# Turning a unit's row maxima on VectorE in 32x32 blocks instead of on TensorE, in a gated attention and MLP kernel

## The chip, the cores and the metric

The kernel runs on one core of a Trainium2 chip. The metric is the device time of one launch in microseconds (us). Before the change it is 2267.89 us, the median of three runs (2267.58 to 2268.26).

## What is computed

The input is 2048 tokens of width 576. A multi-head softmax attention (32 heads of width 18) and an MLP with a LayerNorm ahead of it are computed from the same `x`, and a sigmoid gate mixes them:

```python
x = A_x
g = _sigmoid((x * gate_w).sum(-1, keepdims=True))
# a: softmax attention
q, k, v = ...                       # x @ wqkv, H = 32 heads, Dh = 18
scores = jnp.einsum("bhqd,bhkd->bhqk", q, k) * Dh ** -0.5
p = _softmax(scores, axis=-1)
a = jnp.einsum("bhqk,bhkd->bhqd", p, v) ... @ wo
# b: MLP
y = _layernorm(x, axis=-1)
h = _gelu(jnp.einsum("bsd,df->bsf", y, w1) + b1)
b = jnp.einsum("bsf,fd->bsd", h, w2) + b2
return g * a + (1 - g) * b
```

The change concerns only the softmax: the maximum of each row of `scores`, which is taken off before the exponential.

## The kernel before

**Two passes over the scores.** The kernel works through 32 units. A unit is a pair of heads and one half of the queries: 2 heads, 1024 queries in 8 tiles of 128, and all 2048 keys. The scores of a unit are computed twice. The first pass (`s1_round`, the matmul of line 204) puts 128 queries on the partitions and 512 keys along the row, and VectorE reduces each result to one maximum per query (line 206). A round `(u, r)` is one such tile for both heads; a unit has 32 rounds. The second pass (`s2`, the matmul of line 284) puts 128 keys on the partitions and 512 queries along the row, ScalarE takes the exponential straight from PSUM (line 286), and `pv` multiplies the result with the values (line 313).

**How the maximum gets into the second pass.** The second pass has queries along the row, where a value per query can't be a bias. So it contracts over 56 rows and not 54: the tile `qa` has two more rows per head, 54 and 55 (and 118 and 119 for the second head, which lies from partition 64), that hold minus the maximum, as a rounded part and its remainder, and `ka` has ones there. `s1_finish` makes these values on VectorE (lines 215 to 218) as a tile `nm2` of 128 queries by 32 columns; the columns are head (2), part (2) and query tile (8). They lie down the partitions, and `qa` wants them along a row. The inner function `rows` does that: TensorE turns the 128x32 tile to 32x128 in a PSUM bank (line 222), ScalarE copies it to the SBUF tile `mr` (line 224), and four DMAs, one for each head and part, each move 8 rows of 512 bytes into one row of `qa` (lines 228 to 237, by way of the helper at line 114).

**PSUM.** The bank for the turned tile comes from the pool `ps_s1`, three banks which are otherwise those of the first pass. A matmul of the first pass therefore needs a bank that VectorE has reduced, or, after a turn, that ScalarE has copied. The second pass has two banks of its own (`ps_s2`), the MLP two (`ps_w`), the output of `pv` one.

**The order of the work** is written out by hand. All engines run the instructions in the order in which the program emits them. The main loop goes over 512 steps (unit and key tile `kc`). A step has two halves; each half emits one round of the first pass between the two heads of the second, then a part of the MLP (`fill`: matmuls of lines 553 and 685), and every second step a `pv`. The first pass runs ahead by some steps: the last round of a unit is emitted about four steps ahead of the first `s2` that needs its maxima. The function `run_due` counts slots; `defer(n, fn)` runs `fn` when n more slots have gone by, and most halves and MLP pieces are a slot each. `s1_finish` runs one slot after a unit's last round. In the loop, `rows` is then put in the list `ROWS`, which is emptied right after the next `pv` (lines 1350 to 1352); for the first unit, whose maxima are made ahead of the loop, `rows` is deferred by 8 slots.

**DMA queues.** Nearly all DMAs are issued from SyncE's queue (SP), in program order: a DMA that waits holds back those behind it. While the loads of the next block of normalized input (`load_y`, tile `big`) stand in that queue, which is so for two of the units, the flag `aside` sends the stores of `rows` to ScalarE's queue instead, spread over slots with `defer`.

The names in the rows below: `nm` is `nm2`, `m` the maxima of a unit, `ps` any PSUM bank, `p` and `ring` the buffers of exponentials, `w` the weights' two parts, `x` a raw or accumulated tile, `z` and `zz` the MLP's activations.

Of the kernel before, what the change touches and what calls it, by code (L numbers as in the profile page):

```python
# [9 lines left out]
F32 = mybir.dt.float32  # L10
F32R = mybir.dt.float32r
AF = mybir.ActivationFunctionType
# [5 lines left out]
P = 128  # L18
# [41 lines left out]
def gated_mix_kernel(ctx: ExitStack, tc: tile.TileContext, x, wqkv, wo, w1, b1, w2, b2, gate_w, out):  # L60
    nc = tc.nc
# [18 lines left out]
    ident = const.tile([P, P], F32, name="ident")  # L80
# [12 lines left out]
    asm = ctx.enter_context(tc.tile_pool(name="asm", bufs=2))  # L93
    ps_s1 = ctx.enter_context(tc.tile_pool(name="ps_s1", bufs=NS1, space=PSUM))
# [5 lines left out]
    def psum(pool):  # L100
        return pool.tile([P, TB], F32, name="ps")
# [10 lines left out]
    def dma_r(queue, dst, src):  # L112

        queue.dma_start(dst.bitcast(F32), src)
# [5 lines left out]
    def defer(n, fn):  # L120
        later.append((slot[0] + n, fn))
# [11 lines left out]
    aside = [-1]  # L133

    def run_due(ns=SLOT):

        slot[0] += 1
        now[0] += ns
        if chain and chain[0][0]():
            chain.pop(0)[1]()  # L140
        due = [f for t, f in timed if t <= now[0]]
        timed[:] = [(t, f) for t, f in timed if t > now[0]]
        for f in due:
            f()
        due = [f for s, f in later if s <= slot[0]]
        later[:] = [(s, f) for s, f in later if s > slot[0]]
        for f in due:
            f()
        k = 0
        while k < len(bg):  # L150
            if pool_end[0] - now[0] < bg[k][2] and slot[0] >= bg[k][0]():
                bg.pop(k)[1]()
                k = 0
            else:
                k += 1
# [15 lines left out]
    def load_q(u):  # L171
        pair, half = unit(u)
        qa = QA[u % 3]
        for h in range(2):
            d0 = (2 * pair + h) * DH
            for i, part in enumerate((0, 0, 1)):
                r = 64 * h + i * DH
                dma_r(nc.sync, qa[r:r + DH, :], qk_scr[part, d0:d0 + DH, half * HALF:(half + 1) * HALF])

    def load_k(pair, c0=0, c1=S):  # L180
        ka = KA[pair % 3]
        for h in range(2):
            d0 = D + (2 * pair + h) * DH
            for i, part in enumerate((0, 1, 0)):
                r = 64 * h + i * DH
                dma_r(nc.sync, ka[r:r + DH, c0:c1], qk_scr[part, d0:d0 + DH, c0:c1])

    def load_v(pair):
        nc.sync.dma_start(VT[pair % 2], v_scr[:, :, pair, :].rearrange("k p e -> p k e"))
# [19 lines left out]
    def s1_finish(u):  # L209

        m4 = M4.pop(u)
        nm = asm.tile([P, 2, 8], F32, name="nm")
        nm2 = asm.tile([P, 2, 2, 8], F32, name="nm2")
        nmh = asm.tile([P, 2, 8], F32R, name="nmh")
        nc.vector.tensor_reduce(nm, m4, axis=AX.X, op=ALU.max, negate=True)
        nc.vector.tensor_copy(nmh, nm)
        nc.vector.tensor_copy(nm2[:, :, 0, :], nmh.bitcast(F32))
        nc.vector.tensor_tensor(nm2[:, :, 1, :], nm, nmh.bitcast(F32), op=ALU.subtract)

        def rows():  # L220
            ps = psum(ps_s1)
            nc.tensor.transpose(ps[:32, :P], nm2.rearrange("p a b c -> p (a b c)"), ident)
            mr = asm.tile([32, P], F32R, name="mr", bufs=1)
            nc.scalar.activation(mr, ps[:32, :P], AF.Copy)
            qa = QA[u % 3]
            aside = slot[0] < ybusy[0]

            def store(h, b):
                r = 64 * h + 54 + b
                k = (h * 2 + b) * 8  # L230
                dma_r(nc.scalar if aside else nc.sync,
                      qa[r:r + 1, :].rearrange("o (t n) -> o t n", n=P), mr[k:k + 8, :].bitcast(F32))
            for k in range(4):
                if aside:
                    defer(1 + 2 * k, lambda k=k: store(*divmod(k, 2)))
                else:
                    store(*divmod(k, 2))
        if looped[0]:
            ROWS.append(rows)
        else:  # L240
            defer(8, rows)

    RING = []
    ybusy = [0]
# [28 lines left out]
    def s2(u, kc, qb, around, ns):  # L273

        flush()
        qa, ka = QA[u % 3], KA[UNITS[u][0] % 3]
        n = u * NT + kc
        if n < 2 and qb == 0:
            RING.insert(n, pp.tile([P, 2, 2, TB], F32, name="p"))

        def head(h):
            ps = psum(ps_s2)
            r0 = 64 * h
            nc.tensor.matmul(ps, ka[r0:r0 + 56, kc * P:(kc + 1) * P], qa[r0:r0 + 56, qb * TB:(qb + 1) * TB],  # L284
                             start=True, stop=True)
            nc.scalar.activation(RING[n % 3][:, qb, h], ps, AF.Exp, scale=SCALE)  # L286

        def tail():
            head(1)
            run_due(ns)  # L290
        head(0)
        if around:
            around(1)
            around(0)
            tail()
        else:
            held.append(tail)
# [3 lines left out]
    def pv(n):  # L301

        flush()
        u, kc = divmod(n, NT)
        if kc == 0:
            OB[u] = psum(ps_o)
        v = VT[UNITS[u][0] % 2]
        for c in (n, n + 1):
            for qb in range(2):
                for h in range(2):  # L310
                    r = 32 * (2 * h + qb)
                    k = c % NT
                    nc.tensor.matmul(OB[u][r:r + 32, :], v[:, k, 19 * h:19 * h + 32], RING[c % 3][:, qb, h, :],  # L313
                                     start=(k == 0), stop=(k == NT - 1))
        if kc == NT - 2:
            o_store(u, OB.pop(u))
# [29 lines left out]
    rounds = [(u, r) for u in range(NU) for r in range(NR)]  # L346
    rounds.reverse()

    ROWS = []
    looped = [False]  # L350

    def take_round():
        u, r = rounds.pop()
        head = s1_round(u, r)
        if r == NR - 1:
            defer(1, lambda: s1_finish(u))
        return head

    def next_round():
        if rounds:  # L360
            flush()
            head = take_round()
            for h in range(2):
                head(h)
# [9 lines left out]
    def loop_round():  # L374
        if lent[0]:
            lent[0] = 0
        elif rounds:
            return take_round()
# [447 lines left out]
    with ExitStack() as a:  # L826
# [215 lines left out]
        for tb in range(NB):  # L1042
# [3 lines left out]
            for g, (fn, args) in enumerate(work):  # L1046
                if tb == 0:
                    if g in W_AT:
                        n = W_AT[g]
# [46 lines left out]
                if tb == 2 and g == 13:  # L1096
                    ps = psum(ps_s1)
# [209 lines left out]
    def fill(step, share):  # L1307

        gap = 3 * (step // 2) + share
        t = spent[0]  # L1310
        if over[0] is None and rounds:
            piece[0] = share
            behind[0] = base + (TOTAL - KEPT - base) * step / BARE
            atom()
            run_due(max(spent[0] - t, GAP))
        elif over[0] is None:
            if not bare_at:
                bare_at.extend((gap, spent[0]))
            g0, s0 = bare_at
            stretch(s0 + (TOTAL - s0) * (gap + 1 - g0) / (1.5 * FIN - g0) - spent[0])  # L1320
            run_due(max(spent[0] - t, GAP))
            if not stream:
                stream.append(proj)
                over[0] = gap - (spent[0] == t)
                spent[0] = 0.0
        if over[0] is not None and over[0] < gap:
            filler(PROJ * 122.5 * (gap - over[0]))
            run_due()

    looped[0] = True  # L1330
    for u in range(NU):
        for kc in range(NT):
            step = u * NT + kc
            if kc == 1:
                if u + 2 < NU:
                    load_q(u + 2)
                if u % 2 == 0 and u // 2 + 1 < NPAIR - 1:
                    load_k(u // 2 + 1)
                    load_v(u // 2 + 1)
                elif u == NU - 5:  # L1340
                    load_k(NPAIR - 1)
                elif u == NU - 4:
                    load_v(NPAIR - 1)
            at[0] = step

            s2(u, kc, 0, loop_round(), 462.0)
            if kc % 2:
                fill(step, 1)
            elif step > 0:
                pv(step - 2)  # L1350
                while ROWS:
                    ROWS.pop(0)()
                run_due(2080.0)
                if step <= 2 * LEAD:
                    next_round()
            else:
                fill(step, 2)
            s2(u, kc, 1, loop_round(), 462.0)
            fill(step, 2 if kc % 2 else 0)
# [29 lines left out]
```

## Time and profile before

| | |
|---|---|
| time, median of three runs | 2267.89 us (2267.58 to 2268.26) |
| profiled execution, first to last instruction (its span) | 2265.6 us |
| TensorE (PE) busy | 2245.0 us, 99% |
| VectorE (DVE) busy | 1669.9 us, 74% |
| ScalarE (ACT) busy | 1438.3 us, 63% |
| GpSimd (POOL) busy | 946.7 us, 42% |
| turns on TensorE (line 222) | 32, mean 284 ns |
| copies to `mr` on ScalarE (line 224) | 32, mean 262 ns |
| DMAs `qa<-mr` | 128 of 4 KB: 120 on SP, 8 on ScalarE's queue |
| mean granted TensorE clock | 0.999 |

How to read it: busy is the time in which an engine runs something; matmuls overlap in TensorE's pipeline and their ends are modelled, so that 99% does not say that every matmul starts as early as it could. For the profiled execution the profile gives its span alone; the three timed runs lie about 2.3 us above that. In a row of the timeline stand the start in us, the length in us, the engine, the line, the operation, what it writes and reads, the shape and the count; in brackets the idle time of the engine before it and what ended that. PEld is TensorE's weight load, SPq and ACTq are instructions that issue a DMA from those queues.

### The profile page before, as it was taken

What the parts mean: (1) busy time and instruction counts of PE and PEld (TensorE: products, weight loads), DVE (VectorE), ACT (ScalarE), POOL (GpSimd) and SP (SyncE); (2) the same over time, 40 slices, a digit from 0 to 9 for tenths busy, and PEclk for the clock granted to TensorE, in tenths of its full rate; (3) what the DMA queues carried; (4) which work ended last, traced back from release to release, by engine and by line L of the source; (5) the groups of instructions that cost most, each with busy time, mean ns of one, the idle gap of its engine ahead of it and who ended that gap; (6) DMA issues with size and microseconds to landing.
All of it is one profiled execution on the core that took longest, in us unless ns stands there. A gap on an engine that the chain in (4) does not pass through costs nothing.

```text
span 2265.6 us, 50898 instructions
## 1 busy us (share of the span) xinstructions
PE 2245.0 (99%) x20601; PEld 1645.2 (73%) x20601; DVE 1669.9 (74%) x2921; ACT 1438.3 (63%) x2655; POOL 946.7 (42%) x936
## 2 busy tenths in 40 slices
PE   8999999999999999999999999999999999999999
PEld 7878666777767776777777777777777777777768
DVE  5675877777777787778777777777777777777545
ACT  4223677777776666666666666666667666666661
POOL 4002456566663444443444344434444444444420
PEclk9999999999999999999999999999999999999999
DMA  7755655545473424233274424243365243322355
GB/s 241 259 189 183 192 163 163 171 131 162 139 216 134 150 96 127 98 111 122 88 173 157 119 95 142 80 120 119 122 166 158 98 120 114 106 99 107 116 179 190
DMA packets 160657, 323.61 MB, mean 143 GB/s; under 512 B 56062, under 2 KB 83618, under 8 KB 149586
## 3 DMA queue, kind: packets, MB, share of 16 engines
q1 hardware_dynamic: 156582, 313.57, 44.1%
q10 hardware_dynamic: 3840, 6.78, 0.8%
q8 instruction: 162, 2.65, 0.5%
q14 instruction: 73, 0.60, 0.1%
HBM read 229.07 MB, written 95.16 MB: 143 GB/s over the span
## 4 chain that ended last, share of the span: by engine, by line
PE 91%; DVE 4%; POOL 3%; ACT 2%; DMA 1%; issue 1%; ACTq 0%; POOLq 0%; DVEq 0%
PE ps L313 19%; PE ps L685 19%; PE ps L553 18%; PE ps L284 13%; PE ps L204 10%; PE ps L961 4%; PE ps L1269 2%; PE ps L979 2%; DVE m L206 1%; POOL zz L160 1%; POOL w L160 1%; POOL hl L160 1%; PE ps L876 0%; DMA p<-in_A_wqkv_dram 0%; PE ps L1010 0%
## 5 line engine op out<-in xcount | busy, mean ns | idle before, releaser
L206 DVE TENSOR_REDUCE m<-ps 128x1 f32<-128x512 f32 x2048 | 1301.5, 683 | 311.9 <-PE ps L204 266.1
L286 ACT ACTIVATE p<-ps 128x512 f32<-128x512 f32 x1368 | 743.7, 596 | 361.9 <-PE ps L204 243.4
L284 PE MATMUL ps<-qa,ka 56*128 56x512 f32 x2048 | 709.5, 413 | 3.2 <-ACT p L286 2.4
L204 PE MATMUL ps<-ka,qa 54*128 54x512 f32 x2048 | 652.9, 418 | 4.4 <-DVE m L206 2.2
L685 PE MATMUL ps<-w,hh 64*128 64x288 f32 x4352 | 524.6, 296 | 2.6 <-ACT z L578 1.8
L553 PE MATMUL ps<-big,w 64*128 64x512 f32 x3888 | 517.2, 392 | 0.1
L284 PEld LDWEIGHTS ps<-qa,ka 56*128 56x128 f32 x2048 | 359.6, 184 | 209.6 <-issue 95.0
L160 POOL TENSOR_SCALAR zz<-zz 128x512 f32<-128x512 f32 x272 | 168.6, 620 | 784.4 <-ACT zz L641 700.9
L286 ACT ACTIVATE ring<-ps 128x512 f32<-128x512 f32 x680 | 369.6, 595 | 186.2 <-PE ps L204 129.5
L553 PEld LDWEIGHTS ps<-big,w 64*128 64x128 f32 x3888 | 394.5, 185 | 59.3 <-ACT vt L990 0.3
L685 PEld LDWEIGHTS ps<-w,hh 64*128 64x128 f32 x4352 | 415.3, 186 | 16.0 <-ACT z L578 2.3
L160 POOL TENSOR_TENSOR zz<-zz,z 128x512 f32<-128x512 f32 x280 | 361.5, 1291 | 34.2 <-ACT zz L643 10.5
L204 PEld LDWEIGHTS ps<-ka,qa 54*128 54x128 f32 x2048 | 337.4, 185 | 33.9 <-DVE m L206 14.0
L685 PE MATMUL ps<-w,hl 64*128 64x288 f32 x2176 | 355.5, 292 | 0.0
L313 PE MATMUL ps<-p,vt 128*32 128x512 f32 x2736 | 344.5, 598 | 0.0
L685 PEld LDWEIGHTS ps<-w,hl 64*128 64x128 f32 x2176 | 240.6, 185 | 1.5
L160 POOL TENSOR_TENSOR w<-x,w 128x576 fp32r<-128x576 f32 (+1 forms) x34 | 68.4, 2014 | 298.3 <-ACT w L450 281.2
L313 PEld LDWEIGHTS ps<-p,vt 128*32 128x32 f32 x2736 | 71.4, 109 | 152.4 <-issue 146.3
L160 POOL TENSOR_TENSOR hl<-zz,hh 128x512 fp32r<-128x512 f32 x134 | 174.1, 1299 | 14.4 <-ACT hh L604 3.5
L313 PE MATMUL ps<-ring,vt 128*32 128x512 f32 x1360 | 179.1, 598 | 0.0
L659 DVE SCALAR_TENSOR_TENSOR x<-ps,x 128x288 f32<-128x288 f32 x270 | 110.7, 451 | 82.4 <-PE ps L685 80.2
L961 PE MATMUL ps<-big,wqk 128*128 128x512 f32 x504 | 123.3, 399 | 0.1
(120 smaller groups left out, 1398.6 us busy)
## 6 DMA issues: line engine op xcount, KB each, us to landing
w<-w_scr SPq DMA_DIRECT2D x54, 1152.0 KB
w<-w_scr SPq DMA_DIRECT2D x108, 576.0 KB
w_scr<-w SPq DMA_DIRECT2D x18, 1152.0 KB
w_scr<-w SPq DMA_DIRECT2D x36, 576.0 KB
qa<-qk_scr SPq DMA_DIRECT2D x192, 72.0 KB
ka<-qk_scr SPq DMA_DIRECT2D x90, 144.0 KB
x<-in_B_w_dram SPq DMA_DIRECT2D x34, 288.0 KB
qk_scr<-hh SPq DMA_DIRECT2D x36, 256.0 KB
```

The costliest lines, as they stand in the source:

```text
L160: fn(*args, **kw)
L204: nc.tensor.matmul(ps, qa[r0:r0 + 54, t * P:(t + 1) * P], ka[r0:r0 + 54, kb * TB:(kb + 1) * TB], start=True, stop=True)
L206: nc.vector.tensor_reduce(M4[u][:, h, t, kb:kb + 1], ps, axis=AX.X, op=ALU.max)
L284: nc.tensor.matmul(ps, ka[r0:r0 + 56, kc * P:(kc + 1) * P], qa[r0:r0 + 56, qb * TB:(qb + 1) * TB], start=True, stop=True)
L286: nc.scalar.activation(RING[n % 3][:, qb, h], ps, AF.Exp, scale=SCALE)
L313: nc.tensor.matmul(OB[u][r:r + 32, :], v[:, k, 19 * h:19 * h + 32], RING[c % 3][:, qb, h, :], start=(k == 0), stop=(k == NT - 1))
L553: nc.tensor.matmul(ps[h], wt[w_][r, c, :], Y[s_][r, c, :], start=(k == 0), stop=(k == 26))
L659: nc.vector.scalar_tensor_tensor(dst, ps[nn][:, :ND], 0.5, b2b[:, cs[nn]] if base else dst, op0=ALU.mult, op1=ALU.add)
L685: mm = nc.tensor.matmul(ps[nn][:, :ND], h_[r, tok], w_[p_][r, cs[nn]], start=(k == 0 or bare and k == 3 * G), stop=(k == 6 * G - 1 or bare ...
L961: nc.tensor.matmul(ps, w_[:, c, ms], big[:, s_, :], start=(k == 0), stop=(k == len(prods) - 1))
L979: nc.tensor.matmul(ps[:, :ND], big[:, s_, tok], w_[:, c, cs], start=(k == 0), stop=False)
L1269: nc.tensor.matmul(ps[t, n][:, :ND], OT[b][3][:, s_, tok], w_part(w_, c)[:, cs], start=(c == 0 and k == 0), stop=(c == 4 and k == 1))
```

## The change

`rows` no longer uses TensorE, PSUM or ScalarE. One VectorE instruction turns `nm2` in four blocks of 32x32: partition 32k + c of `mr` then holds column c for the 32 queries of block k. A row of `qa` is put together from these blocks by eight DMAs in place of four: the store (h, k) moves 16 partitions of 128 bytes, both parts and all 8 query tiles of one head and one block, into two rows of `qa`. In the loop, `rows` is deferred by two slots after `s1_finish` and no longer waits for the next `pv`; the list `ROWS` is gone. Where the stores go to ScalarE's queue they stand one slot apart, slots 1 to 8, where they stood two apart, slots 1 to 7.

```diff
         def rows():
-            ps = psum(ps_s1)
-            nc.tensor.transpose(ps[:32, :P], nm2.rearrange("p a b c -> p (a b c)"), ident)
-            mr = asm.tile([32, P], F32R, name="mr", bufs=1)
-            nc.scalar.activation(mr, ps[:32, :P], AF.Copy)
+            mr = asm.tile([P, 32], F32, name="mr", bufs=1)
+            nc.vector.transpose(mr, nm2.rearrange("p a b c -> p (a b c)"))
             qa = QA[u % 3]
             aside = slot[0] < ybusy[0]
 
-            def store(h, b):
-                r = 64 * h + 54 + b
-                k = (h * 2 + b) * 8
-                dma_r(nc.scalar if aside else nc.sync,
-                      qa[r:r + 1, :].rearrange("o (t n) -> o t n", n=P), mr[k:k + 8, :].bitcast(F32))
-            for k in range(4):
+            def store(h, k):
+                r = 64 * h + 54
+                c = 32 * k + 16 * h
+                dst = qa[r:r + 2, :].rearrange("b (t k n) -> b t k n", k=4, n=32)[:, :, k, :]
+                dma_r(nc.scalar if aside else nc.sync, dst, mr[c:c + 16, :])
+            for n in range(8):
                 if aside:
-                    defer(1 + 2 * k, lambda k=k: store(*divmod(k, 2)))
+                    defer(1 + n, lambda n=n: store(*divmod(n, 4)))
                 else:
-                    store(*divmod(k, 2))
-        if looped[0]:
-            ROWS.append(rows)
-        else:
-            defer(8, rows)
+                    store(*divmod(n, 4))
+        defer(2 if looped[0] else 8, rows)
...
-    ROWS = []
...
                 pv(step - 2)
-                while ROWS:
-                    ROWS.pop(0)()
                 run_due(2080.0)
```

On TensorE the 32 turns are all that changes; every other instruction stands where it stood. The place is the 30th unit whose maxima are turned, at 2011.29 us of the profile. Before, on TensorE (`qa_104` and `ka_108` belong to the unit in the second pass, `qa_103` to the one in the first):

```order
L313 MATMUL ps<-ring_2268,vt_109 32x512 x4
L313 MATMUL ps<-p,vt_109 32x512 x4
L222 MATMUL ps<-ident,nm_29156 32x128
L284 MATMUL ps<-qa_104,ka_108 128x512
L204 MATMUL ps<-ka_108,qa_103 128x512 x2
L284 MATMUL ps<-qa_104,ka_108 128x512
```

In the changed kernel the row of line 222 is missing and the others are the same. On VectorE at the same unit, before:

```order
L218 TENSOR_TENSOR nm_29156<-nm,nmh 128x2x8
L206 TENSOR_REDUCE m_29177<-ps 128x1 x8
L577 TENSOR_SCALAR z<-ps,b1t 128x512
L206 TENSOR_REDUCE m_29177<-ps 128x1 x8
L659 SCALAR_TENSOR_TENSOR x<-ps,x 128x288 x2
```

and in the changed kernel (its line numbers are a little lower behind line 237):

```order
L218 TENSOR_TENSOR nm_29214<-nm,nmh 128x2x8
L206 TENSOR_REDUCE m_29235<-ps 128x1 x2
L222 STREAM_TRANSPOSE mr<-nm_29214 128x32
L206 TENSOR_REDUCE m_29235<-ps 128x1 x6
L571 TENSOR_SCALAR z<-ps,b1t 128x512
L206 TENSOR_REDUCE m_29235<-ps 128x1 x8
```

The turn stands two reductions behind the last value of `nm2`; in other units it stands right behind two additions of line 659. On ScalarE, in the first of the two units whose stores go to its queue (at 677.30 us), before:

```order
L224 ACTIVATE mr<-ps 32x128
L114 DMA qa_104<-mr 1x8x128
L286 ACTIVATE p<-ps 128x512 x2
L114 DMA qa_104<-mr 1x8x128
L286 ACTIVATE p<-ps 128x512 x2
L114 DMA qa_104<-mr 1x8x128
L286 ACTIVATE p<-ps 128x512 x2
L114 DMA qa_104<-mr 1x8x128
L286 ACTIVATE ring_2268<-ps 128x512 x4
```

and in the changed kernel, where line 281 is the exponential:

```order
L114 DMA qa_104<-mr 2x8x32 x2
L281 ACTIVATE p<-ps 128x512 x2
L114 DMA qa_104<-mr 2x8x32 x2
L281 ACTIVATE p<-ps 128x512 x2
L114 DMA qa_104<-mr 2x8x32 x2
L281 ACTIVATE p<-ps 128x512 x2
L114 DMA qa_104<-mr 2x8x32 x2
L281 ACTIVATE ring_2268<-ps 128x512 x4
```

Two issues stand between pairs of exponentials where one stood. On SP the stores of the other 30 units stay at their place in the queue, eight for four.

## The prediction

> **What bounds the kernel now.** I read the page first: the busy shares and the chain that ended last.
>
> ```profile
> PE 2245.0 (99%) x20601; PEld 1645.2 (73%) x20601; DVE 1669.9 (74%) x2921; ACT 1438.3 (63%) x2655; POOL 946.7 (42%) x936
> ...
> PE 91%; DVE 4%; POOL 3%; ACT 2%; DMA 1%; issue 1%; ACTq 0%; POOLq 0%; DVEq 0%
> ```
>
> TensorE is busy for 99% of the span and makes 91% of the chain. To see whether that holds in the stages where the turns stand, I took the windows; after the stretch, each row has the stretch's length, then the busy time of PE, PEld, DVE, ACT and POOL.
>
> ```profile
> 250.00:700.00 450.00, 444.42 (x4241) 314.96 (x4237) 344.27 (x589) 329.72 (x600) 265.94 (x235) 1.00 0.52 158
> ...
> 1200.00:1700.00 500.00, 499.80 (x4868) 359.54 (x4860) 387.29 (x669) 334.80 (x626) 214.53 (x227) 1.00 0.40 122
> ```
>
> From 700 us on TensorE leaves nothing free (0.2 us in 500); from 250 to 700 us it leaves 5.6 us. So time taken from TensorE's stream should come off the end nearly in full, and time put on another engine costs only where TensorE ends up waiting. Which engines the change touches, the groups say (line, engine, operation, count, then busy time and mean ns, then idle time before them):
>
> ```profile
> L222 PE MATMUL ps<-ident,nm 128*32 128x128 f32 x32 | 9.1, 284 | 0.0
> L224 ACT ACTIVATE mr<-ps 32x128 fp32r<-32x128 f32 x32 | 8.4, 262 | 23.7 <-PE ps L222 23.7
> ```
>
> The 9.1 us are a busy time of overlapping matmuls, not what the turns cost. That is read from starts: how much later does the next work start when a turn stands between? In TensorE's timeline, a `pv` with no turn behind it:
>
> ```profile
> 1013.04 1.04 PE L313 MATMUL ps<-p,vt 128*32 128x512 f32 x8
> 1014.01 0.50 PE L284 MATMUL ps<-qa,ka 56*128 56x512 f32 x1
> ...
> 1014.59 0.39 PE L553 MATMUL ps<-big,w 64*128 64x512 f32 x2
> ```
>
> The last block of the `pv` starts at 1013.04, the second pass 0.97 us later, the MLP 0.58 us after that. The next one, with a turn:
>
> ```profile
> 1041.84 1.04 PE L313 MATMUL ps<-ring,vt 128*32 128x512 f32 x8
> 1042.81 0.28 PE L222 MATMUL ps<-ident,nm 128*32 128x128 f32 x1
> 1043.03 0.50 PE L284 MATMUL ps<-qa,ka 56*128 56x512 f32 x1
> ...
> 1043.60 0.30 PE L685 MATMUL ps<-w,hh 64*128 64x288 f32 x2
> ```
>
> Here the second pass starts 1.19 us after the block, so the turn takes 0.22 us; the rest, 0.57 us, is as without it. And a dearer one:
>
> ```profile
> 2010.32 1.04 PE L313 MATMUL ps<-p,vt 128*32 128x512 f32 x8
> 2011.29 0.28 PE L222 MATMUL ps<-ident,nm 128*32 128x128 f32 x1
> 2011.50 0.50 PE L284 MATMUL ps<-qa,ka 56*128 56x512 f32 x1
> ...
> 2012.55 0.39 PE L553 MATMUL ps<-big,w 64*128 64x512 f32 x2
> ```
>
> Again about 0.2 us for the turn, but then 1.05 us to the MLP and not 0.58. The timeline with all engines names the reason; the first and the last of these places, weight load of the first pass's second matmul:
>
> ```profile
> 366.85 0.18 PEld L204 LDWEIGHTS ps<-ka,qa 54*128 54x128 f32 x1 [0.41 <-DVE m L206]
> ...
> 2012.21 0.18 PEld L204 LDWEIGHTS ps<-ka,qa 54*128 54x128 f32 x1 [0.42 <-DVE m L206]
> ```
>
> The turned tile holds one of the three `ps_s1` banks, so the second matmul of the round waits for VectorE to free another. I read the same rows at all 32 turns: 31 stand behind a `pv` as here, and nine of them have this wait.
>
> **What the change takes from TensorE.** 31 turns by 0.22 us are 6.8 us. Nine bank waits by 1.05 - 0.58 = 0.47 us are 4.2 us. Together 11.0 us. The 32nd turn, the first in time, stands ahead of the main loop, and I cost it at nothing, for TensorE stands still there soon after in any case:
>
> ```profile
> 243.07 1.27 DVE L206 TENSOR_REDUCE m<-ps 128x1 f32<-128x512 f32 x2
> 245.84 2.83 SPq L114 DMA_DIRECT2D qa<-mr  x4
> 249.06 0.74 PE L685 MATMUL ps<-w,hh 64*128 64x288 f32 x4 [1.84 <-ACT z L578]
> 250.98 0.62 PE L284 MATMUL ps<-qa,ka 56*128 56x512 f32 x1
> ```
>
> At 249.06 it has waited 1.84 us for ScalarE, whatever came before.
>
> **What it puts on VectorE.** 32 turns of 128x32. The trace has no such operation. The nearest are a copy of 16 columns, a reciprocal of 16, and at the far end the reduction of 512 (in the first two rows the three numbers are the shortest, median and longest in ns):
>
> ```profile
> L217 DVE COPY nm<-nmh x32: 174/175/1265, 240.0 to 2131.4; 128x16 f32<-128x16 f32 x32
> L336 DVE RECIPROCAL dn<-dn x32: 240/242/254, 341.3 to 2215.6; 128x16 f32<-128x16 f32 x32
> L206 DVE TENSOR_REDUCE m<-ps 128x1 f32<-128x512 f32 x2048 | 1301.5, 683 | 311.9 <-PE ps L204 266.1
> ```
>
> I take 0.22 us, near the small ones, bounds 0.17 and 0.68. Only the Trainium skill has a figure for the operation itself: "VectorE: DVE Perf Modes", section "The three transpose paths", gives 311 ns for 128x128 in bf16, four times our columns; the sum below would not move by more than 0.8 us with it. No run shown here has the operation.
>
> VectorE is 74% busy and the turn runs in its gaps, except where TensorE waits for the reductions behind it. That is at the nine tight places: there the bank is free now, but every reduction behind the turn ends 0.22 us later. Some 0.1 us of that is covered, since the second matmul comes 0.3 us behind the first; I take 0.1 us given back at nine places, 1.0 us, with 0 as the lower end and as the upper one 0.57 us (a turn as long as a reduction) at nine, 5.1 us.
>
> **What it takes from ScalarE.** The copies, 8.4 us, and the 23.7 us in which ScalarE stood ahead of them waiting for the turn. TensorE hardly waits for ScalarE:
>
> ```profile
> L284 PE MATMUL ps<-qa,ka 56*128 56x512 f32 x2048 | 709.5, 413 | 3.2 <-ACT p L286 2.4
> ```
>
> So this is worth between 0 and 3.2 us. I take 0.
>
> **The stores on SP.** Eight issues for four in 30 units. An issue in the trace and its neighbour with still smaller pieces (64 bytes each):
>
> ```profile
> L114 SPq DMA_DIRECT2D qa<-mr x120: 625/635/1454, 245.8 to 2136.5; - x120
> L327 SPq DMA_DIRECT2D dn<-oe x32: 584/602/623, 320.5 to 2212.6; - x32
> ```
>
> 128 pieces of 64 bytes cost no more to issue than 8 of 512, so I take the same price for 16 of 128: 2.83/4 = 0.71 us from one issue to the next, 5.7 us for eight. In the first unit the whole train had landed within 250.98 - 248.67 = 2.3 us of its last issue, as TensorE did not wait at 250.98. So the rows are there 8.0 us after `mr`. The tightest unit of the loop:
>
> ```profile
> 1893.13 2.70 SPq L114 DMA_DIRECT2D qa<-mr  x4
> ...
> 1904.38 0.39 PE L284 MATMUL ps<-qa,ka 56*128 56x512 f32 x1
> ```
>
> SP starts as `mr` is ready, and 1904.38 is the unit's first matmul of the second pass (a unit has 64, counted from the first): 11.3 us of room, 3.3 us to spare. `mr` should also be ready earlier, since the turn stands two reductions behind `nm2` and waits for no `pv`. Only the first unit has less room: `mr` at about 243.07 + 1.27 + 0.22 = 244.6 us, landed by 252.6 us at the latest against 250.98. I take 0.5 us, bounds 0 and 1.6.
>
> Behind the stores, loads on SP come 2.8 us later. The one used soonest:
>
> ```profile
> 494.77 1.36 SPq L418 DMA_DIRECT2D x<-in_B_w_dram  x2
> ...
> 508.12 0.69 ACT L450 ACTIVATE w<-x 128x576 fp32r<-128x576 f32 x1
> ```
>
> Its reader follows 13.4 us behind the issue. Nothing.
>
> **The stores on ScalarE's queue**, in two units. There an issue keeps the next exponential from being sent off:
>
> ```profile
> 677.60 1.23 ACTq L114 DMA_DIRECT2D qa<-mr  x1
> 678.92 0.67 ACTq L114 DMA_DIRECT2D qa<-mr  x1
> 679.52 0.50 PE L284 MATMUL ps<-qa,ka 56*128 56x512 f32 x1 [0.25 <-ACT p L286]
> ```
>
> The first store waits for VectorE's turn, as ScalarE's copy now waits for TensorE's, with the exponentials queued behind it either way. Four issues cost TensorE 0.25 us. Four more per unit, two in a row between exponentials, cost 0.25 us again, 0.5 us in both; at most their whole length, 8 by 0.63 = 5.0 us; below, the present 0.25 us could go. The Trainium skill, "DMA: Bandwidth & Descriptors", section "Issuing engines are not separate DMA queues", calls the sequencer's time for issuing usually small beside the DMA; by it this term would be 0 and the forecast 0.5 us lower. The 0.25 us above speak against that here.
>
> **Sum.** 11.0 - 1.0 - 0.5 - 0.5 = 9.0 us off the profiled execution, whose span is 2265.6 us; the median of the runs is 2.3 us above that span, and I take the same difference off it: 2267.9 - 9.0 = 2258.9 us, 0.4%. About 0.2%, 4.5 us, can be told from no change here.
>
> **Rivals.**
>
> 1. *The bank wait stays, with VectorE as its cause.* At the nine places VectorE, not the lost bank, sets when the round's second matmul can start; 4.2 us stay. For it: the wait is named after VectorE's reduction, and the change adds to VectorE's queue just there. Against it: at the other 22 places the same queue makes no such wait. Then 11.0 - 4.2 - 1.0 = 5.8 us off: 2262.1. With a turn near a reduction's length also 1.0 us more: 2263.1.
>
> 2. *The saving is taken back by the next wait.* In the stretch from 250 to 700 us TensorE waits 5.6 us for others, so the seven units there might give nothing, 7 by 0.35 = 2.5 us; and the two units with stores on ScalarE's queue could lose their full 5.0 us. Both together leave 9.0 - 2.5 - 4.5 = 2.0 us: 2265.9, no change. The full windows after 700 us speak against it.
>
> 3. *The rows land late (slower).* If an issue or its landing is paid by the piece, sixteen pieces for eight, the step is 1.42 us and eight take 11.3 us; with 2.3 us to land that is 13.6 us against 11.3. It decides from 1.13 us a step. TensorE would stand 1.8 us (room of 11.8 us, a more usual unit) in 30 units, 54 us less 11: about 2311 us. The Trainium skill, "DMA: Bandwidth & Descriptors", section "Specifications", names 512 bytes as the least for full rate, with a read-modify-write below, which speaks for this; its section "Why small descriptors are slow (HBM only)" excepts transfers within SBUF. Against it: the 602 ns of the 64-byte pieces.
>
> 4. *The change doesn't do what it says*, for instance VectorE's turn waiting on the last unit's eight stores. The two bank waits shown, at 366.85 and 2012.21, are 27 units apart, 61 us from one unit to the next, so those stores landed long ago; I give it no chance of its own.
>
> **How the numbers follow.** Forecast 0.75, rival 1 0.10 (faster by just over 0.2% or just under it, half each), rival 2 0.09, rival 3 0.06. Faster 0.75 + 0.05 = 0.80, same 0.05 + 0.09 = 0.14, slower 0.06. The terms' bounds: at best 11.0 + 3.2 + 0.5 = 14.7 us off, 2253.2; the forecast's own costs all at their upper ends give 11.0 - 5.1 - 5.0 - 1.6, no gain. For 8 in 10 I leave out the ends where several bounds meet and rival 3, and take in rival 1: 2255.0 to 2264.5.
>
> **What would show it.** Right: line 222 gone from PE; in all units 0.97 us from the `pv`'s last block to the second pass and about 0.58 to the MLP; VectorE's turn at 0.2 to 0.3 us; no wait for `qa<-mr` on PE; PE's busy time lower by some 10 us. Wrong: waits of L204 for VectorE at more than a few units (rival 1), waits of L284 for ScalarE near 677 and 1165 us (rival 2), issues of `qa<-mr` above 1.1 us and L284 waiting for them (rival 3).

## The result and the profile after

The changed kernel takes 2254.64 us (median of four runs, 2254.17 to 2255.61), the kernel before beside it 2268.05 us (2267.58 to 2268.26): a ratio of 0.9943, 95% interval 0.9930 to 0.9955, 13.4 us less. The forecast was 9.0 us less, 2258.9 us, with a range of 2255.0 to 2264.5: the measured time lies 0.4 us below the lower end of the range. Timed once more beside the later experiments, the two take 2254.55 and 2267.22 us, ratio 0.9943 (0.9931 to 0.9956), 12.7 us.

The page of the changed kernel, its span and busy times:

```profile
span 2253.3 us, 51099 instructions
...
PE 2231.5 (99%) x20569; PEld 1649.5 (73%) x20569; DVE 1671.8 (74%) x2953; ACT 1431.6 (64%) x2623; POOL 946.2 (42%) x936
```

TensorE has 32 instructions fewer and 13.5 us less busy time (2245.0 before), VectorE 32 more and only 1.9 us more. Now the tile `mr` (number, then shortest, median and longest in ns, then first and last start):

```profile
L222 DVE STREAM_TRANSPOSE mr<-nm x32: 193/201/203, 242.0 to 2121.7; 128x32 f32<-128x32 f32 x32
L114 SPq DMA_DIRECT2D qa<-mr x240: 596/611/1226, 242.2 to 2126.7; - x120
L114 ACTq DMA_DIRECT2D qa<-mr x16: 617/621/1244, 673.7 to 1165.7; - x16
```

VectorE's turn takes 0.20 us, as forecast (0.22). A store of 16 pieces of 128 bytes costs no more to issue than one of 8 pieces of 512 (in the median 611 ns, 635 ns before). No engine waited for `qa<-mr`, in the first unit neither. The place that stood at 1041.84 before, with a turn behind the `pv`:

```profile
1036.33 1.04 PE L308 MATMUL ps<-ring,vt 128*32 128x512 f32 x8
1037.30 0.50 PE L279 MATMUL ps<-qa,ka 56*128 56x512 f32 x1
...
1037.88 0.43 PE L679 MATMUL ps<-w,hh 64*128 64x288 f32 x4
```

It is 0.97 us to the second pass and 0.58 to the MLP, as where no turn stood. The dear place of 2010.32:

```profile
1999.73 1.04 PE L308 MATMUL ps<-p,vt 128*32 128x512 f32 x8
2000.70 0.50 PE L279 MATMUL ps<-qa,ka 56*128 56x512 f32 x1
...
2001.34 1.09 PE L547 MATMUL ps<-big,w 64*128 64x512 f32 x8
```

These are 0.97 and 0.64 us, where it was 1.18 and 1.05: the turn is gone, and nearly all of the bank wait.

To see all places, I laid the TensorE instructions of two traces side by side in order, without the turns. At each of the 31 places behind a `pv` I took two intervals: from the `pv`'s last matmul to the second pass, and from there to the MLP. Their sums, in us, here for all kernels of the study that the text speaks of (each is explained below):

| kernel | to the second pass | to the MLP |
|---|---|---|
| before | 22.9 | 21.8 |
| changed | 16.2 | 18.4 |
| e_pad | 16.2 | 18.5 |
| e_turn | 22.9 | 17.5 |
| e_slot | 16.2 | 25.3 |
| e_turnslot | 22.9 | 22.1 |
| e_dve4 | 16.2 | 21.5 |
| e_now | 18.1 | 20.0 |

Without any wait the second column is 17.5 (30 places by 0.575, the last 0.24). So the change took 22.9 - 16.2 = 6.7 us for the turns (forecast 6.8); the waits of the second column were 21.8 - 17.5 = 4.3 us (forecast 4.2) and are 0.9 us now (forecast 1.0). That makes 10.1 us. The same comparison shows 1.4 us more spent up to 237 us in the kernel before, where no instruction was moved. That was the first open question.

### The profile page after: what moved, and what is told of

It reads as the page before. It is cut to its first block, busy times and chain, and to the rows that moved or that the text cites. A ratio compares the mean times of both kernels' runs of the same rounds, so it can differ in the third digit from the quotient of the medians.

```text
span 2253.3 us, 51099 instructions
## 1 busy us (share of the span) xinstructions
PE 2231.5 (99%) x20569; PEld 1649.5 (73%) x20569; DVE 1671.8 (74%) x2953; ACT 1431.6 (64%) x2623; POOL 946.2 (42%) x936
## 4 chain that ended last, share of the span: by engine, by line
PE 92%; POOL 3%; DVE 2%; ACT 2%; DMA 1%; issue 0%; SPq 0%; ACTq 0%; DVEq 0%; POOLq 0%
PE ps L308 20%; PE ps L679 19%; PE ps L547 18%; PE ps L279 14%; PE ps L204 11%; PE ps L955 4%; PE ps L1263 3%; PE ps L973 2%; POOL zz L160 1%; POOL hl L160 1%; POOL w L160 1%; DVE m L206 1%; PE ps L870 0%; DMA p<-in_A_wqkv_dram 0%; ACT p L281 0%
## 5 line engine op out<-in xcount | busy, mean ns | idle before, releaser
L547 PEld LDWEIGHTS ps<-big,w 64*128 64x128 f32 x3888 | 401.6, 185 | 51.9 <-ACT vt L984 0.4
L679 PEld LDWEIGHTS ps<-w,hh 64*128 64x128 f32 x4352 | 421.7, 186 | 15.9 <-ACT z L572 2.1
L679 PE MATMUL ps<-w,hl 64*128 64x288 f32 x2176 | 364.8, 292 | 0.0
L679 PEld LDWEIGHTS ps<-w,hl 64*128 64x128 f32 x2176 | 246.4, 185 | 1.4
```

What stands on the lines that cost most here:

```text
L547: nc.tensor.matmul(ps[h], wt[w_][r, c, :], Y[s_][r, c, :], start=(k == 0), stop=(k == 26))
L679: mm = nc.tensor.matmul(ps[nn][:, :ND], h_[r, tok], w_[p_][r, cs[nn]], start=(k == 0 or bare and k == 3 * G), stop=(k == 6 * G - 1 or bare ...
```

## The experiments

The theory to test: the gain is 31 turns taken off TensorE and banks given back, and what is put on VectorE, SP and ScalarE's queue is hidden but for about 2 us. The rival: a part of the gain is from elsewhere (the rows' time, ScalarE, the start of the program). In the diffs, `old place` stands for the list `ROWS`, put back where the kernel before had it.

**The turn alone, the bank alone, both.** The first, `e_turn`, puts back TensorE's turn, into the bank that the next first-pass matmul then overwrites:

```diff
+    def dead_turn(nm2, keep):
+        ps = psum(ps_s1)
+        nc.tensor.transpose(ps[:32, :P], nm2.rearrange("p a b c -> p (a b c)"), ident)
+        if keep:
+            PRE.append(ps)          # s1_round: ps = PRE.pop() if PRE else psum(ps_s1)
...
+            ROWS.append(lambda: dead_turn(nm2, True))       # old place
```

> The changed kernel with the TensorE turn put back at its old place behind the pv, in 31 units, and nothing else: its result is not read, and it is written into the bank that the next first-pass matmul takes in any case, so that no bank is lost. Theory (the gain is turns taken off TensorE plus banks given back): the turns alone cost 31 x 0.21 = 6.6 us, so 2254.6 + 6.6 = 2261 us, and no more waits of the first pass for VectorE than in the changed kernel. Rival (most of the gain is from elsewhere: rows made earlier, ScalarE freed, the start of the program): at most 3 us, 2257 to 2258.

Measured: 2259.02 us, 4.4 us over the changed kernel, between the two. The dear place in its trace:

```profile
2002.37 1.04 PE L318 MATMUL ps<-p,vt 128*32 128x512 f32 x8
2003.34 0.28 PE L213 MATMUL ps<-ident,nm 128*32 128x128 f32 x1
2003.56 0.50 PE L289 MATMUL ps<-qa,ka 56*128 56x512 f32 x1
...
2004.13 1.10 PE L558 MATMUL ps<-big,w 64*128 64x512 f32 x8
```

The turn costs its 0.22 us again, but the MLP follows 0.57 us later and not 0.64: while TensorE turns, VectorE catches up. In the table the first column is that of before (22.9) and the second falls to 17.5, no wait at all. So the net is 6.7 - 0.9 = 5.8 us at the places, and not 6.6. The run shows only 4.4: side by side with a second profile of the changed kernel (`e_after`, below), 0.6 to 0.9 us comes back between the places and 0.8 behind the last one, which was not followed up.

The second, `e_slot`, takes the bank alone out of turn:

```diff
+            ROWS.append(lambda: nc.vector.memset(psum(ps_s1)[:, :1], 0.0))   # old place
```

> The changed kernel with one bank of the first pass's pool taken out of turn at the old place of the turn, in 31 units: a one-column memset on VectorE stands in it, TensorE has nothing added. Theory: the lost bank makes the waits, nine units by 0.35 to 0.47 us, so 3.2 to 4.2 us more, 2258 to 2259, and the waits of the first pass for VectorE are back at the nine places. Rival (VectorE's own queue made the waits): within 1 us of 2254.6.

Measured: 2260.14 us, 5.5 us over the changed kernel, more than either expected. At the dear place, TensorE and then its weight loads:

```profile
2004.55 1.04 PE L310 MATMUL ps<-p,vt 128*32 128x512 f32 x8
2005.52 0.49 PE L281 MATMUL ps<-qa,ka 56*128 56x512 f32 x1
...
2006.76 1.09 PE L550 MATMUL ps<-big,w 64*128 64x512 f32 x8
```

```profile
2006.42 0.18 PEld L204 LDWEIGHTS ps<-ka,qa 54*128 54x128 f32 x1 [0.41 <-DVE m L206]
```

It is 1.24 us to the MLP, where the kernel before had 1.05. The wait for VectorE's reduction comes from the lost bank, and rival 1 of the prediction is out; it is longer than before, probably since no turn runs ahead of it (the memset's own 0.06 us on VectorE is in it too).

`e_turnslot` has both: the `dead_turn` above with `keep` false.

> The changed kernel with the TensorE turn back at its old place and in a bank of its own of the first pass's pool, in 31 units; nothing reads it and ScalarE has no copy. Theory: both parts together, 6.6 + 3.3 = 9.9 us, 2264.5 us, and the two single experiments add up to this one. What then still lacks to the kernel before, 3.5 us, must be ScalarE's copy, the place of the rows or the start of the program. Rival (the freed ScalarE makes up half the gain or more): 2261 or less.

Measured: 2263.93 us, 9.3 us over the changed kernel. Its two columns are those of before (22.9 and 22.1). From `e_turn` to `e_turnslot` only the bank changes, with no work added on VectorE: 4.9 us more, and the second column goes from 17.5 to 22.1. That is the cleaner test of the bank. The theory holds for the sum; the parts overlap (11.6 us singly against 9.5 together, at the 31 places as far as the fourth second-pass matmul behind each).

**All the old work and all the new.**

```diff
+    def old_way(nm2):
+        ps = psum(ps_s1)
+        nc.tensor.transpose(ps[:32, :P], nm2.rearrange("p a b c -> p (a b c)"), ident)
+        mo = asm.tile([32, P], mybir.dt.bfloat16, name="mo", bufs=1)
+        nc.scalar.activation(mo, ps[:32, :P], AF.Copy)
...
+            ROWS.append(lambda: old_way(nm2))               # old place
```

> The kernel before with all the new work on top: TensorE's turn and ScalarE's copy at their old place (the copy now writes a bf16 tile that nobody reads), in 31 units, and beside them VectorE's turn and the eight stores of the changed kernel. Theory: what is new costs 1 to 2 us (VectorE's turn at the tight units, the stores on ScalarE's queue in two units), so 2268 + 1.5 = 2269.5 us. Rival (the new work is free, and its earlier rows even help): 2266 to 2268. If it is under 2265, something else than the turn, its bank and its copy made part of the gain.

Measured: 2264.59 us, 0.7 us over `e_turnslot`, so ScalarE's copy costs next to nothing; but also 3.2 us *under* the kernel before (2267.77 beside these four), though it does all that one does and more. By its own last sentence, something else made part of the gain.

**Is it the one execution?** The kernel before, once more.

> The kernel before once more, unchanged, with a second profile. In the first profile of before the same TensorE instructions ahead of 243 us, where no turn stands yet, run 1.1 to 1.3 us slower than in all five profiles taken since (396 ns instead of 391 ns for the 128x512 matmuls from 176 to 196 us). If that belongs to the one execution, this profile has 391 ns and a span of about 2264.5 us; if it belongs to the program, 396 ns and 2265.6 us again. The ratio to itself should be 1.000 within 0.001.

Measured: 2267.65 us, ratio 1.000 (0.9991 to 1.0009). The projections' matmuls from 177 to 195 us, in the first profile of before and, the same to the digit, in this one:

```profile
L961 PE MATMUL ps<-big,wqk 128*128 128x512 f32 x79 | 18.6, 396 | 0.0
```

So it belongs to the program. The span doesn't come out as expected: it is 2267.8 us and not 2265.6. Laid side by side, the two executions of this one kernel differ by 1.1 us in the first 20 us and by 0.9 near 250 us, so a difference of 2 us between two single profiles says little until it is placed.

No instruction differs from 177 to 195 us between the two kernels. What differs is where data lie: `mr` was 32 partitions of 512 bytes and is 128 of 128 bytes, and SBUF is given out by bytes per partition. In the compiled programs every tile allocated behind it, the weights of the projections and of the MLP among them, lies 384 bytes lower (`wqk` at byte 149,344, before 149,728; in `e_all` at 149,600), while the other operand of these matmuls, `big`, has not moved.

**The old layout, the new instructions.**

```diff
-            mr = asm.tile([P, 32], F32, name="mr", bufs=1)
+            mr = asm.tile([P, P], F32, name="mr", bufs=1)[:, :32]
```

> The changed kernel with mr 512 bytes wide in each partition, as it was before, and only its first 128 bytes used: no instruction moves, but what lies behind mr in SBUF lies 384 bytes further, as before the change. In both profiles of before the 128x512 matmuls of the projections (176 to 196 us) take 396 ns, in seven of the changed kernel and its variants 391 ns. Theory (the 396 ns come from where the data lie): 396 ns again, and 1.0 to 1.3 us more, 2255.6 to 2256. Rival (they come from the instructions, of which there are fewer kinds or others): 391 ns and 2254.6.

Beside it the changed kernel, with no edit:

> The changed kernel once more, unchanged, beside the other three on the same chip: 2254.6 us within 0.7, the measure for what the others show.

Measured: `e_pad` 2258.43 us (2256.61 to 2259.45), `e_after` 2254.55 us (2254.07 to 2255.05): 3.9 us between them, three times the expected size. The same stretch and then the MLP's first matmuls in the whole kernel, first of `e_pad`:

```profile
L955 PE MATMUL ps<-big,wqk 128*128 128x512 f32 x78 | 18.4, 396 | 0.0
...
L547 PE MATMUL ps<-big,w 64*128 64x512 f32 x3888 | 516.9, 392 | 0.1
```

and of `e_after`:

```profile
L955 PE MATMUL ps<-big,wqk 128*128 128x512 f32 x80 | 18.5, 391 | 0.0
...
L547 PE MATMUL ps<-big,w 64*128 64x512 f32 x3888 | 513.6, 390 | 0.2 <-ACT vt L984 0.2
```

The instructions are the same, in the same order. With the weights at their old place the projections take 396 ns again. The expectation counted only the start; laid side by side, `e_after` leads `e_pad` by 1.5 us at 237 us, by 2.0 at 317 and by 3.6 at 2146. The 0.5 us between 237 and 317 is not the layout: in the profile of `e_pad` TensorE has a granted clock of 0.50, half the full one, from 252.5 to 255.9 us, in that of `e_after` 1.00. The first profile of the changed kernel has 6.8 us of this near 250 us, and loses 0.9 us there to `e_after`, the same program. So the layout is worth about 3 us: 1.5 ahead of the loop and 1.6 in it, where the MLP's weights have moved, and its tiles `z` and `zz` with them. Which of these tiles counts in the loop no run separates.

Against the kernel before, `e_pad` is 8.8 us faster (0.9960, 0.9947 to 0.9972): that is what the change does by itself. The profiles of both have 3.4 us at half the clock near 250 us.

**VectorE's price.**

```diff
-            nc.vector.transpose(mr, nm2.rearrange("p a b c -> p (a b c)"))
+            for _ in range(4):
+                nc.vector.transpose(mr, nm2.rearrange("p a b c -> p (a b c)"))
```

> The changed kernel with VectorE's turn made four times over (three times for nothing): 3 x 0.2 = 0.6 us more on VectorE in each unit. Theory: VectorE's time costs only at the tight units, where the first pass waits for a reduction; there are nine to fourteen of these, so 9 x 0.5 to 14 x 0.6 = 4.5 to 8.4 us more, 2259 to 2263. Rival (VectorE has room everywhere, its 26% of idle time): under 1 us. Rival (VectorE's time is TensorE's time in all units): 18.6 us, 2273.

Measured: 2263.17 us, 8.6 us more, the upper end of the theory. Of 31 x 0.6 = 18.6 us more on VectorE, about half shows. The idle time ahead of line 204's weight loads and matmuls that ended with a reduction of VectorE, in the changed kernel and then in this one (us, times):

```profile
  DVE m L206: 13.0, 24
```

```profile
  DVE m L206: 26.9, 44
```

There are twenty more waits, 13.9 us longer in sum (weight loads and matmuls overlap, so that is not the time lost). VectorE's 26% of idle time is no room for work at a fixed place.

**The turn earlier.**

```diff
-        defer(2 if looped[0] else 8, rows)
+        if looped[0]:
+            rows()
+        else:
+            defer(8, rows)
```

> The changed kernel with the rows made at once, right behind the last value of nm, and not two slots later (in the loop; the first unit as before). VectorE then has the turn ahead of two reductions or additions more, away from the tight place behind the pv. Theory: the 1 us that is left of waits of the first pass behind the pv goes in part, and the same time may be lost elsewhere: 2253.6 to 2255.1. Rival (the two slots matter, since the earlier turn delays the last reductions that TensorE waits for): 1 us or more slower.

Measured: 2258.60 us, 4.0 us more: the rival. VectorE at the dear place, in the changed kernel (TensorE waits for the two reductions at 2000.27):

```profile
1998.41 0.22 DVE L215 TENSOR_REDUCE nm<-m 128x16 f32<-128x64 f32 x1
1998.67 0.97 DVE L216 CAST nmh<-nm 128x16 fp32r<-128x16 f32 x1
1999.68 0.17 DVE L217 COPY nm<-nmh 128x16 f32<-128x16 f32 x1
1999.76 0.59 DVE L218 TENSOR_TENSOR nm<-nm,nmh 128x16 f32<-128x16 f32 x1
2000.27 1.27 DVE L206 TENSOR_REDUCE m<-ps 128x1 f32<-128x512 f32 x2
2001.47 0.19 DVE L222 STREAM_TRANSPOSE mr<-nm 128x32 f32<-128x32 f32 x1
```

In `e_now` the turn stands ahead of these reductions, and TensorE's weight load behind them waits:

```profile
2003.26 0.21 DVE L222 STREAM_TRANSPOSE mr<-nm 128x32 f32<-128x32 f32 x1
2003.40 3.72 DVE L206 TENSOR_REDUCE m<-ps 128x1 f32<-128x512 f32 x6
```

```profile
2004.10 0.18 PEld L204 LDWEIGHTS ps<-ka,qa 54*128 54x128 f32 x1 [0.34 <-DVE m L206]
```

The turn behind the two reductions costs this place nothing; ahead of them it costs its 0.2 us. The rows also say what makes the place tight: the four operations that make `nm2` take 1.9 us, since the cast takes 0.97. Its usual time is 0.18, and GpSimd's row beside it ends when it ends:

```profile
L216 DVE CAST nmh<-nm x32: 174/176/991, 238.0 to 2119.6; 128x16 fp32r<-128x16 f32 x32
```

```profile
1998.33 1.28 POOL L160 TENSOR_TENSOR zz<-zz,z 128x512 f32<-128x512 f32 x1
```

I read the four operations of all 32 units beside GpSimd's, in the traces of both kernels. At all nine tight places one of them is drawn out to the end of such a GpSimd instruction (the four then take 1.0 to 2.0 us), at twenty of the other 23 they take 0.7 to 0.8. The Trainium skill, "SBUF — State Buffer", section "SBUF: two separate sides", has a port pair of SBUF that VectorE and GpSimd share as an exclusive lock: the one that starts first holds it for its whole instruction, and the other waits. The trace agrees: the drawn-out operation ends 0.03 us behind GpSimd's. VectorE's turn is never drawn out (at most 216 ns in any run, that in `e_dve4`). Of the 3.5 us that `e_now` has more in the table's columns, 1.9 come from another place, at 677 us, in the first unit with its stores on ScalarE's queue: the second pass waits there for an exponential. The turns account for the other 1.6 us at the places, not for the whole 4.0 us. Part of those is the clock again: `e_now` has 6.8 us at half the clock near 250 us and loses 1.2 us to `e_after` there.

**The turn later.** In `e_defer3`, and with 4 in `e_defer4`:

```diff
-        defer(2 if looped[0] else 8, rows)
+        defer(3 if looped[0] else 8, rows)
```

> The changed kernel with the rows one slot later (three slots behind the last maxima and not two). In 14 units VectorE's turn then stands behind two reductions more, in the rest where it was. One slot earlier than now cost 4 us, since the turn stood ahead of reductions that TensorE waits for. Theory (two slots already let those reductions go first where it matters; what is left, 1 us at the tight places, is VectorE's own backlog): within 0.7 us of the changed kernel. Rival (the later the better, as long as the rows are in time): 0.7 to 2 us faster.

> The same with four slots: the turn goes behind two more reductions in most units. The rows are then made about 2 us later than in the changed kernel; the last of eight stores is issued 4.8 us behind the turn and, by the sixteen stores, lands 2.6 us after that, 7.4 us against the 10.9 us of the tightest unit less 2: still in time, with 1.5 us to spare. Theory: the turn no longer stands ahead of a reduction that the place behind the pv waits for, up to 1 us faster. Rival (rows late, or the turn ahead of the next reductions that are waited for): slower by 1 us or more.

Measured: 2256.92 and 2254.51 us. Four slots are as good as two (2254.55), so nothing beats the changed kernel here. Three slots cost 2.4 us against the theory's 0.7, but not by VectorE (the five executions lie between 2256.04 and 2258.87, and the profiled one is the longest). In that profile 3.8 us go in one unit, that of 1160 us, whose stores are on ScalarE's queue. There, first ScalarE's queue, then TensorE:

```profile
1164.75 0.62 ACTq L114 DMA_DIRECT2D qa<-mr  x1
```

```profile
1173.14 0.47 PE L279 MATMUL ps<-qa,ka 56*128 56x512 f32 x1 [1.99 <-DMA qa<-mr]
1173.54 1.83 PE L308 MATMUL ps<-p,vt 128*32 128x512 f32 x8
```

TensorE still waits for a store 8.4 us after the last was issued. That wait is 2.0 of the 3.8 us. The eight matmuls behind it take 1.83 us, where they take 1.04 elsewhere, and the window says why; the third number from the end is the granted clock:

```profile
1173.70:1177.10 3.40, 3.40 (x18) 0.53 (x10) 0.00 (x0) 0.55 (x1) 0.00 (x0) 0.50 0.81 166
```

If half the clock means half the work, 3.4 us of it lose about 1.7 us, which is most of the other 1.8 us. With four slots the last issue there stands at 1166.0 and TensorE waits for none of them; why the stores land so late in one kernel was not found.

**More stores.**

```diff
             def store(h, k):
-                r = 64 * h + 54
-                c = 32 * k + 16 * h
-                dst = qa[r:r + 2, :].rearrange(...)[:, :, k, :]
-                dma_r(nc.scalar if aside else nc.sync, dst, mr[c:c + 16, :])
+                for b in range(2):
+                    r = 64 * h + 54 + b
+                    c = 32 * k + 16 * h + 8 * b
+                    dst = qa[r:r + 1, :].rearrange(...)[:, :, k, :]
+                    dma_r(nc.scalar if aside else nc.sync, dst, mr[c:c + 8, :])
```

> The changed kernel with sixteen stores of 8 pieces in place of eight of 16: twice as many issues, the same pieces. Theory (an issue costs the same whatever its pieces, and the stores lie beside other work): a step of 0.69 us as with eight, so the last store is issued 15 x 0.69 = 10.3 us behind the turn and lands 1.7 us later, 12.0 us against 11.8 us of room for the second head in the tightest units: 0 to 2 us more, 2255 to 2257. Rival (an issue is paid by the piece): a step of 0.35 us, and no time at all, 2254.6. Rival (the rows of the eight stores land late already): each unit 5.5 us later, over 2300.

Measured: 2288.93 us, 34.3 us more. The issues in one unit, and TensorE's waits in the whole kernel (us, times, longest):

```profile
L114 SPq DMA_DIRECT2D qa<-mr x16: 625/629/698, 308.0 to 318.1; - x16
```

```profile
PE ps L280 <- ACT p L282: 9.9, 11, 2.6
PE ps L280 <- DMA qa<-mr: 7.9, 5, 3.6
...
PE ps L680 <- DMA w<-w_scr: 4.2, 2, 2.3
```

The step is 10.1/15 = 0.67 us: half the pieces, the same price, so an issue is not paid by the piece, and rival 3 of the prediction falls. But the expectation of 0 to 2 us was far too low. Side by side with the changed kernel, 5.4 us go in the first unit, 4.7 and 5.1 in the two whose stores are on ScalarE's queue, 7.6 at 1679 us of the changed kernel (1704 to 1715 us here), and the rest in steps of 0.3 to 1.6 us at the tight units. Of the 7.6 us, 4.2 are the two waits for the MLP's weights, whose loads stand behind the stores on SP. The other 3.4 are half of a stretch of 6.8 us at half the clock:

```profile
1708.10:1714.90 6.80, 6.25 (x46) 5.97 (x48) 2.58 (x4) 3.20 (x6) 0.00 (x0) 0.50 0.30 121
```

At one of the tight units the second head's matmul starts 1.56 us late, 11.2 + 1.56 = 12.8 us behind the turn. The last store is issued 10.6 us behind the turn there, so it lands within 2.2 us of its issue, against the 1.7 that I had taken from the first unit and the 2.3 of the prediction. Eight stores then need 7 x 0.67 + 2.2 = 6.9 us, and the tightest unit has 10.9: they are hidden, with 4.0 us to spare.

## Why the prediction was right, and where it was not

The change by itself was forecast at 9.0 us and is 8.8 (`e_pad` against before). The other 3.9 to 4.6 us were not in the prediction: about 3 are the layout, and the rest is of the size by which executions of one kernel differ. The span of `e_pad` is 8.9 us below that of before. Side by side these are: 0.1 before the first turn, 0.6 in the first unit, 9.9 at the 31 places, -1.2 between them, -0.5 at the end. That 8.8 falls so near 9.0 is partly luck, for errors of the sum nearly cancel: the first unit gave 1.1 us more than forecast, and between the places and at the end 1.2 us more were lost.

- *31 turns by 0.22 us, 6.8*: right, 6.7. `e_turn` shows the cause.
- *Nine bank waits by 0.47, 4.2*: right in size, 4.3 over all places (some are smaller than 0.47 and stand outside the nine). `e_slot`, and `e_turnslot` against `e_turn`, show that the lost bank makes them. Turns and banks are not independent terms, though: TensorE's turn hid a part of the bank wait, which the plain sum doesn't say. It came out since both went together.
- *VectorE gives back 1.0*: right in size, 0.9 of waits are left, wrong in part in its cause. At five of the nine tight places the turn stands behind the two reductions that TensorE waits for, as at 2000.27, and costs nothing there. At the other four (489, 674, 976 and 1578 us) it stands right ahead of them, as the prediction had it, and the most wait is left there, 0.12 to 0.20 us each. One slot later, in `e_defer3`, these four lose 0.06 to 0.12 us each, and the second column falls to 17.9. The rest stands where VectorE was held up in making `nm2`; that this delay, which TensorE's 0.22 us no longer cover, is its cause is argued and not tested.
- *The first unit, 0*: it gave 0.6 us.
- *ScalarE's copies, 0*: 0.7 us at most (`e_all` less `e_turnslot`), not told from nothing.
- *The stores on SP, 0, and 0.5 late in the first unit*: no matmul waits for them, the first unit's neither; the step is 0.67 us and not 0.71, the landing 1.7 to 2.2 us. In `e_pad` one weight load of the first unit waits 0.3 us for them.
- *The stores on ScalarE's queue, 0.5*: of the 1.2 us lost between the places, 0.6 lie in the second of the two units, none in the first. The page of the Trainium skill that the prediction weighed ("DMA: Bandwidth & Descriptors", "Issuing engines are not separate DMA queues") calls such a cost usually small; `e_now`, `e_defer3` and `e_16` show waits of TensorE of 1.8 to 2.6 us in such a unit. The remaining 0.6 us, in the two units from 305 to 428 us, were not followed up.

What failed is the step that is not there: the parts were costed as instructions removed, added and moved, and "the 32 turns are all that changes" on TensorE was taken to mean that its other instructions run as before. The smaller tile moved the weights in SBUF, and the same matmuls became 0.5 to 1.3% shorter (392 to 390 and 396 to 391 ns). That the layout is the cause is shown by `e_pad`; that it is the weights' own place is argued from what moved, and why these addresses are faster is open.

## What to carry to other kernels

On a full engine, price a removed instruction by the starts around it, and test each part alone: a wait that the instruction hid comes out when it goes. An idle share is no room; new work on a shared engine costs nothing only behind what the full engine waits for, and a turn of 0.2 us ahead of it cost up to 0.2 us each time here. A long wait of the full engine can cost more than its length: read the granted clock behind it. Two versions that differ in the size of one tile differ in the addresses of all behind it: pad the tile back before a difference of some 0.2% is put down to the instructions.

## What was not expected of the hardware

- The layout of SBUF changes TensorE's pace: 396 ns with `wqk` at byte 149,728 (three profiles), 391 ns 128 bytes lower (`e_all`) and 384 bytes lower (ten profiles of the changed kernel and its variants); about 3 us in 2255 in all.
- Issues of 8 pieces of 512 bytes, 16 of 128 and 8 of 128 cost 635, 611 and 635 ns in the median: neither bytes nor pieces matter here.
- A turn of 128x32 in blocks of 32x32 takes 0.20 us on VectorE, about what a copy of 16 columns takes (0.17), and never more than 0.216, while a cast, copy or subtraction of 16 columns beside a GpSimd TENSOR_TENSOR takes up to 1.3.
- Stretches with TensorE at half the clock (granted 0.50), 3.4 or 6.8 us long, stand near 250 us in most profiles (13.7 us in `e_16`) and not in those of `e_after` and `e_turn`. Between these and the last microseconds of the kernel they come only in `e_defer3` and `e_16`, beside waits of TensorE of 1.9 to 2.6 us; at the 1.8 us wait of `e_now` at 675.8 us there is none. What brings them on was not tested.
